# Causal scores in 64x64 tiles without their empty blocks: what it does to a retention and expert kernel

## The chip, the cores and the metric

The kernel runs on one core of one Trainium2 chip. The metric is the device time of one execution in microseconds (us). Three runs of the kernel before took 401.07, 401.35 and 401.92 us; the median is 401.35.

## The reference, cut to what matters

Retention (linear attention with a decay per head) is followed by a mixture of experts with one expert per token. Only the retention is touched by the change.

```
B, H, S, D = 4, 8, 768, 64
gamma = 1 - 2 ** (-5 - arange(H)); scale = 1 / sqrt(D)
for t in range(S):
    state = gamma * state + k[:, :, t] (outer) v[:, :, t]
    y[:, :, t] = scale * q[:, :, t] @ state
...
x = y as (3072 tokens, 512)
expert of a token = argmax(x @ w_gate + bias of its modality)
out = gate * relu(x @ w1[expert]) @ w2[expert]
```

Within a stretch of 128 tokens, y of token t is the part that comes from the state before the stretch, and the sum over the tokens s <= t of the stretch of (q_t . k_s) v_s with decays. The matrix of these scores is zero for s > t: a causal mask.

## The kernel before, in words

The 3072 tokens are 24 chunks of 128 (six per batch, so chunk n starts a batch where n % 6 == 0 and ends one where n % 6 == 5). All operands are fp32; an fp32 matmul is two instructions on TensorE (PE). For each chunk the kernel runs these steps, all with 8 heads of 64, held as 4 groups g of two heads j:

- `load_kq`, `load_kv` (L119 to L140): 512 KB each, q and k with features on the partitions, and k and v with tokens on the partitions. SyncE (SP) issues them some ten chunks ahead.
- `decay_v` (L152): v times a decay on GpSimd (POOL). `decay_q` (L142): a decay for the output on ScalarE (ACT), four instructions.
- `scores` (L161): k^T q for each head, a 64x128 tile (64 rows of the array, 128 columns) with 128 moving columns, into two PSUM banks, one for each j; then VectorE (DVE) multiplies each bank by the mask and writes it to `abuf` (L173).
- `heads_s` (L183): the state's part of y, 64x64 tiles (L192). `heads_a` (L197): the scores' part, added in the same PSUM tiles, 128x64 tiles with 128 moving columns (L204); then DVE writes `yT` (L211).
- `tokens_out` (L213): y back to token rows and the gate logits in one matmul with 128x128 tiles (L221), copied by ACT to `xs` (L225), logits summed by DVE into `lg` (L226).
- `state` (L230): k^T v added to the state in a PSUM tile that lives as long as the batch, 128x64 tiles (L240), copied by ACT.

PSUM has 8 banks here, all from one pool with one tag (`bank`, L78); a new tile takes a bank whose last tile is released, and waits until that tile's readers are done. PE, ACT, DVE and SP run their instructions in the order in which the program writes them (`manual_schedule`, L1055).

The order around the change: `one_chunk` handles chunks 0 and 1, `first_pair` prepares chunks 2 and 3, and `two_chunks(n)` (L899) handles n and n+1 for n = 2, 4, ... 22. In it the scores and the state of the next pair are made, and `tokens_out` of the last pair. Other work is put between the steps by hooks (`at`, `run`): `run(n, "end")` after the tokens, for example, runs what was put there.

- In chunks 6, 12 and 18, at "end": `route_a` parts 0 and 1 (L312), the routing of the six chunks before, a row of small DVE instructions (L316 to L340).
- In chunks 7, 13 and 19, at "end": `route_b`, `route_c`, `route_a` part 2 (rank matmul, positions, gates), in 13 also `early_a` and `early_b` (L455 to L487: DVE picks the two experts that start early).
- In the two chunks after that, six `scatter`s on POOL (L366), one instruction after the other, each with an indirect DMA.
- In chunk 14: `taken_a` at "st" (DVE writes `tk`), `taken_b` at "end" (PE matmuls `ptk`, L497, that read `tk`).
- In chunks 18 and 20, at "end": `cut` (L669), a weight block split in two by ACT (`hi_e`) and DVE (`lo_e`, L677). In chunks 20 and 22: `flip`, transposes on PE for the first expert job.

After the attention, six jobs of experts follow (`first` L692, `second` L711), 192 matmuls of 128x512 each.

## Time and profile before

| What | Before |
|---|---|
| Median of three runs | 401.35 us |
| Profiled execution | 402.62 us, of which span 400.8 us |
| PE busy | 383.6 us, 96% of the span |
| DVE, ACT, POOL busy | 47%, 39%, 24% |
| Scores on PE (L168) | 27.7 us, 384 instructions, mean 293 ns |
| Scores' part of y on PE (L204) | 27.5 us, 384 instructions, mean 290 ns |
| Mask product on DVE (L173) | 30.0 us, 48 instructions, mean 681 ns |
| First expert matmul (L698) starts | 111.87 us |

Times in a timeline are microseconds from the start of the span. Matmuls are pipelined, so one instruction's length (some 0.3 us) is much longer than the step from one to the next. A row of the timeline gives the start, the length of the whole block, engine, line, operation, what is written from what, the tile form as rows*columns of the array, the shape of the moving operand and the count; in brackets, the idle time before it and what ended that. In the answer on stretches of the span, each engine has its busy time and, in parentheses, its instruction count; then come the clock granted to PE, the share of the DMA engines and GB/s.

### The profile page before, as it was taken

The page shows a single profiled execution, that of the slowest core. Times are in us where ns is not written, and L with a number is a line of the kernel's source. Part 1 is how long each engine was busy: PE and PEld are TensorE (multiplying, and loading weights), DVE is VectorE, ACT ScalarE, POOL GpSimd, SP SyncE. Part 2 cuts the span into 40 slices and gives each one's busy share as a digit, 9 for nine tenths or more (in the row PEclk, how much of TensorE's full clock was granted, in tenths as well). Part 3 has the DMA queues.
Part 4 walks back from the last instruction along what each step waited for, and adds up shares of the span by engine and source line. Part 5 has one row for each costly group of instructions (what it writes and reads, how often), then busy time and mean ns, then how long its engine had stood idle before and what let it go on. Part 6 is the DMA issues. An engine that isn't in the chain of part 4 may idle for free.

```text
span 400.8 us, 8169 instructions
## 1 busy us (share of the span) xinstructions
PE 383.6 (96%) x3067; PEld 323.2 (81%) x3067; DVE 187.8 (47%) x434; ACT 155.6 (39%) x305; POOL 96.7 (24%) x140
## 2 busy tenths in 40 slices
PE   4999999799999999999999999999999999999993
PEld 3999888698887888888877888878888888888882
DVE  1676858768649952445223352233622463234200
ACT  1255535336845432345223452334523443243110
POOL 1342581832810875000110001100011000100010
PEclk9999999899999999999999999999999999999999
DMA  7999899794545759367952579525343443400011
GB/s 273 398 385 398 303 339 400 239 390 174 198 147 189 248 184 330 116 216 243 370 201 81 198 243 359 214 71 199 105 159 105 156 166 131 151 35 0 15 39 50
DMA packets 27947, 82.32 MB, mean 205 GB/s; under 512 B 4861, under 2 KB 4989, under 8 KB 27649
## 3 DMA queue, kind: packets, MB, share of 16 engines
q1 hardware_dynamic: 22336, 66.09, 47.4%
q0 software_dynamic: 5136, 15.21, 9.8%
q8 instruction: 26, 0.43, 0.4%
q10 hardware_dynamic: 432, 0.46, 0.4%
q14 instruction: 17, 0.14, 0.1%
HBM read 65.42 MB, written 23.41 MB: 222 GB/s over the span
## 4 chain that ended last, share of the span: by engine, by line
PE 46%; issue 32%; DMA 12%; POOL 4%; DVE 3%; ACT 1%; POOLq 1%; SPq 0%; ACTq 0%
PE h_e L698 11%; PE o_e L716 11%; DMA kq<-in_qkv_dram 6%; DMA kv<-in_qkv_dram 6%; PE h_f L698 6%; PE o_f L716 5%; PE x L221 4%; POOL out_dram L730 3%; PE y L204 2%; PE sc L168 2%; PE y L192 1%; PE st L240 1%; PE xp_f L683 1%; PE xp_e L683 1%; DVE yT L211 1%
## 5 line engine op out<-in xcount | busy, mean ns | idle before, releaser
L698 PE MATMUL h_f<-xT_f,hi_f 128*128 128x512 f32 x256 | 81.3, 393 | 0.0
L716 PE MATMUL o_f<-hi_f,hT_f 128*128 128x512 f32 x256 | 79.4, 391 | 0.0
L677 DVE TENSOR_TENSOR lo_f<-raw_f,hi_f 128x1024 fp32r<-128x1024 f32 x32 | 39.2, 1224 | 49.5 <-ACT hi_f L672 45.3
L698 PEld LDWEIGHTS h_f<-xT_f,hi_f 128*128 128x128 f32 x256 | 48.1, 188 | 11.1 <-issue 1.2
L716 PEld LDWEIGHTS o_f<-hi_f,hT_f 128*128 128x128 f32 x256 | 47.6, 188 | 9.6
L706 DVE SCALAR_TENSOR_TENSOR hT_f<-h_f,hT_f 128x512 fp32r<-128x512 f32 x32 | 22.2, 692 | 66.4 <-ACT hT_f L705 66.4
L698 PE MATMUL h_f<-xT_f,lo_f 128*128 128x512 f32 x128 | 49.9, 390 | 0.0
L716 PE MATMUL o_f<-lo_f,hT_f 128*128 128x512 f32 x128 | 49.9, 390 | 0.0
L730 POOL DMA_INDIRECT out_dram<-o_f,tok_f x16 | 15.6, 972 | 132.6 <-ACT o_f L729 117.8
L698 PE MATMUL h_e<-xT_e,hi_e 128*128 128x512 f32 x128 | 40.5, 392 | 0.0
L705 ACT ACTIVATE hT_f<-h_f 128x512 fp32r<-128x512 f32 x32 | 19.2, 599 | 54.9 <-PE h_f L698 54.9
L716 PE MATMUL o_e<-hi_e,hT_e 128*128 128x512 f32 x128 | 39.8, 392 | 0.0
L173 DVE TENSOR_TENSOR abuf<-sc,cst 128x512 f32<-128x512 f32 x48 | 30.0, 681 | 17.4 <-PE sc L168 17.4
L156 POOL TENSOR_TENSOR vd<-kv,cst 128x512 f32<-128x512 f32 x24 | 24.9, 1045 | 42.5 <-PE y L204 13.5
L672 ACT CAST hi_f<-raw_f 128x1024 fp32r<-128x1024 f32 x32 | 33.4, 1045 | 0.0
L168 PE MATMUL sc<-kq 64*128 64x128 f32 x384 | 27.7, 293 | 5.4 <-DMA kq<-in_qkv_dram 5.2
L729 ACT ACTIVATE o_f<-o_f,gate_f 128x512 f32<-128x512 f32 x15 | 10.3, 689 | 55.0 <-PE o_f L716 43.6
L168 PEld LDWEIGHTS sc<-kq 64*128 64x128 f32 x384 | 24.6, 199 | 7.3 <-DMA kq<-in_qkv_dram 5.2
L221 PE MATMUL x<-wgt,yT 128*128 128x136 f32 x192 | 26.6, 287 | 3.1 <-DVE abuf L173 2.9
L225 ACT COPY xs<-x 128x272 f32<-128x272 f32 x48 | 18.4, 388 | 26.3 <-PE x L221 18.8
L716 PEld LDWEIGHTS o_f<-lo_f,hT_f 128*128 128x128 f32 x128 | 24.0, 188 | 5.0
L698 PEld LDWEIGHTS h_e<-xT_e,hi_e 128*128 128x128 f32 x128 | 24.0, 188 | 4.9
(172 smaller groups left out, 536.7 us busy)
## 6 DMA issues: line engine op xcount, KB each, us to landing
raw_f<-in_w_dram SPq DMA_DIRECT2D x32, 512.0 KB, 3.5
kq<-in_qkv_dram SPq DMA_DIRECT2D x23, 512.0 KB, 8.1
kv<-in_qkv_dram SPq DMA_DIRECT2D x19, 512.0 KB, 9.6
raw_e<-in_w_dram SPq DMA_DIRECT2D x16, 512.0 KB, 4.4
xg_f<-xsl SPq DMA_DIRECT2D x16, 272.0 KB, 4.4
abuf<-in_w_dram SPq DMA_DIRECT2D x8, 512.0 KB, 6.8
rw<-in_w_dram SPq DMA_DIRECT2D x16, 256.0 KB, 5.4
xg_e<-xsl SPq DMA_DIRECT2D x8, 272.0 KB, 4.2
```

The lines of the kernel that those rows point to most:

```text
L156: nc.gpsimd.tensor_tensor(vds[n], vv, dec[:, n % NCH].unsqueeze(2).to_broadcast([P, H, D]), op=ALU.mult)
L168: nc.tensor.matmul(pe[j][:, g * P : (g + 1) * P], kt[r, g], qt[r, g], start=True, stop=True, skip_group_check=True,)
L173: nc.vector.tensor_tensor(a[:, j], pe[j].rearrange("p (h t) -> p h t", t=P), mask.unsqueeze(1).to_broadcast([P, NG, P]), op=ALU.mult,)
L221: nc.tensor.matmul(px[:, g], yT[:, 2 * u + g], wgt[:, 2 * u + g], start=(g == 0), stop=(g == 1), skip_group_check=True,)
L225: nc.scalar.copy(xs[:, 2 * u : 2 * u + 2], px)
L672: nc.scalar.copy(hi, t)
L677: nc.vector.tensor_tensor(lo, t, hi.bitcast(F32), op=ALU.subtract)
L698: nc.tensor.matmul(s.ph, s.w[1][f // 2][wi][:, o : o + P], s.xT[kc][a], start=(kc == 0 and k == 0), stop=(kc == KC - 1 and k == 2),)
L705: nc.scalar.activation(hi, s.ph, AF.Relu)
L706: nc.vector.scalar_tensor_tensor(lo, s.ph, 0.0, hi.bitcast(F32), op0=ALU.max, op1=ALU.subtract)
L716: nc.tensor.matmul(s.po, s.hT[f][a][:, hh * P : (hh + 1) * P], s.w[2][f // 2][wi][:, (f % 2) * DM : (f % 2 + 1) * DM], start=(f == 0 and k ...
L730: ins = nc.gpsimd.indirect_dma_start(out=out[:, :], out_offset=bass.IndirectOffsetOnAxis(ap=s.tok[:, hh : hh + 1], axis=0), in_=o[:, :], i ...
```

## The change

Each head's 128x128 score matrix is cut into 64x64 blocks; the block of late k and early q is zero and is no longer made. For one head, k's early half gives 64 rows with 128 columns, k's late half 64 rows with 64 columns. So that the two heads of a pair of groups fill a bank together, some heads (`turned`) have their token halves exchanged: on the partitions of the scores, and in v, k and the decays with tokens on the partitions, which the host lays out so. Two heads share 192 columns (`AW`): 64 columns with the early blocks of both (low), then 64 for each head with all 128 rows (high). The mask product has 2 x 192 columns in place of 512. The scores' part of y is then made in two steps: `heads_lo`, 64x64 tiles with 64 columns, and `heads_hi`, 128x64 tiles with 64 columns. Heads are placed differently in the y tiles (partition half by g // 2, column by g % 2), and constants and gate weights follow.

[...]

The order of `two_chunks` changes: both `scores` move behind `tokens_out` and the hooks at "end"; the second one stands between the first and the second half of `heads_lo`. The forms of PE's tiles in a pair are then 128x128, 64x64, 128x64; before they were 64x128, 128x128, 64x64, 128x64.

```diff
     def scores(n):
         kt, qt = (kqs[n][:, i].rearrange("p (g t) -> p g t", g=NG) for i in range(2))
...
+        for late in range(2):
+            for u in range(2):
+                for j in range(2):
+                    r = slice(j * D, (j + 1) * D)
+                    for g in (2 * u, 2 * u + 1):
+                        w = turned(g, j)
+                        o = pe[j][(late + w) % 2 * HP : ((late + w) % 2 + 1) * HP, u]
+                        qs = qt[r, g]
...
+                        nc.tensor.matmul(
+                            o, kt[r, g, late * HP : (late + 1) * HP], qs,
+                            start=True, stop=True, skip_group_check=True,
+                        )
         for j in range(2):
             nc.vector.tensor_tensor(
+                a[:, j], pe[j], mask.unsqueeze(1).to_broadcast([P, 2, AW]), op=ALU.mult
             )
...
+    def heads_lo(n, c):
...
+        for j in range(2):
+            for g in (c, c + 2):
+                w = turned(g, j)
+                r = slice(w * HP, (w + 1) * HP)
+                h = slice(g // 2 * D, (g // 2 + 1) * D)
+                ins = nc.tensor.matmul(
+                    py[j][h, c, :HP], vd[r, 2 * g + j], a[r, j, g // 2, :HP],
+                    start=(first and c == 0), stop=(c == 1), skip_group_check=True,
+                )
+                if c and seen:
+                    tc.add_manual_dep(ins.ins, seen.pop().ins.name, synced, reason="PSUM banks")
+
+    def lo_seen(n):
+        seen.append(nc.scalar.copy(sight, pys[n][1][HP : HP + 1, 0, :1]))
+
+    def heads_hi(n):
...
+        for j in range(2):
+            for g in (0, 2, 1, 3):
+                w = turned(g, j)
+                h = slice(g // 2 * D, (g // 2 + 1) * D)
                 nc.tensor.matmul(
+                    py[j][h, g % 2, HP:], vd[:, 2 * g + j],
+                    a[:, j, g // 2, (1 + w) * HP : (2 + w) * HP],
+                    start=False, stop=(g % 2 == 1), skip_group_check=True,
                 )
...
@@ two_chunks
         decay_q(n)
-        if ahead:
-            scores(n + 2)
         run(n, "st")
         if ahead:
-            scores(n + 3)
             decay_v(n + 3)
...
             tokens_out(n - 1)
-        decay_q(n + 1)
         run(n, "end")
         run(n + 1, "top")
+        if ahead:
+            scores(n + 2)
         if n % NCH:
             heads_s(n)
+        heads_lo(n, 0)
         heads_s(n + 1)
+        heads_lo(n + 1, 0)
+        lo_seen(n + 1)
         run(n + 1, "st")
-        heads_a(n)
+        decay_q(n + 1)
+        if ahead:
+            scores(n + 3)
+        heads_lo(n, 1)
+        heads_lo(n + 1, 1)
+        heads_hi(n)
+        heads_out(n)
+        run(n + 1, "sc")
         if ahead:
             state(n + 2)
-        run(n + 1, "sc")
-        heads_a(n + 1)
+        heads_hi(n + 1)
+        heads_out(n + 1)
         run(n + 1, "pr")
         if ahead:
             state(n + 3)
@@ one_chunk
         state(n)
         decay_q(n)
         run(n, "st")
-        scores(n + 1)
...
             heads_s(n)
-        heads_a(n)
+        heads_lo(n, 0)
+        lo_seen(n)
+        scores(n + 1)
+        heads_lo(n, 1)
+        heads_hi(n)
+        heads_out(n)
         run(n, "end")
```

`heads_out` holds the two DVE instructions that write yT. `heads_s` keeps its matmuls and goes through the groups as 0, 2, 1, 3.

## The prediction

> **What bounds the kernel now.** I read the page first, then the stretches of the span, the waits before TensorE (PE), and PE's timeline of one pair of chunks.

> ```profile
> PE 383.6 (96%) x3067; PEld 323.2 (81%) x3067; DVE 187.8 (47%) x434; ACT 155.6 (39%) x305; POOL 96.7 (24%) x140
> 120.00:200.00 80.00, 80.00 (x373) 65.98 (x372) 42.88 (x112) 32.46 (x47) 25.81 (x33) 1.00 0.69 237
> 20.00:30.00 10.00, 10.00 (x178) 9.21 (x178) 7.46 (x15) 5.77 (x19) 4.72 (x6) 1.00 1.02 385
> PE sc L168 <- DMA kq<-in_qkv_dram: 5.2, 1, 5.2
> PE x L221 <- DVE abuf L173: 2.9, 1, 2.9
> kq<-in_qkv_dram SPq DMA_DIRECT2D x23, 512.0 KB, 8.1
> ```

> PE is busy for 96% of the span, and for all of 120 to 200 us in the experts' stage, so a microsecond that attention wins or loses reaches the end whole. Its one wait for a load is the first; the queues are then full (a share of 1.02 at 385 GB/s), but a pair needs two chunks of two 512 KB loads, 5.4 us, which still fits under a pair of 7. Its longest wait for another engine is 2.9 us, on VectorE (DVE). So I price PE's work first, and then ask which waits the new order makes.

> ```profile
> 26.27 2.06 PE L168 MATMUL sc<-kq 64*128 64x128 f32 x32
> 28.26 2.12 PE L221 MATMUL x<-wgt,yT 128*128 128x136 f32 x16
> 30.31 1.10 PE L192 MATMUL y<-kq,s 64*64 64x128 f32 x32
> 31.34 1.09 PE L204 MATMUL y<-abuf,vd 128*64 128x128 f32 x16
> 33.60 0.64 PE L240 MATMUL st<-vd,kv 128*64 128x64 f32 x16
> 34.17 0.38 PE L168 MATMUL sc<-kq 64*128 64x128 f32 x2
> ...
> 18.06 1.16 PE L168 MATMUL sc<-kq 64*128 64x128 f32 x16
> 19.15 1.19 PE L221 MATMUL x<-wgt,yT 128*128 128x136 f32 x8
> 38.20 0.67 PE L192 MATMUL y<-kq,s 64*64 64x128 f32 x16
> 109.03 1.97 PE L204 MATMUL y<-abuf,vd 128*64 128x128 f32 x32
> 64.20 0.63 PE L240 MATMUL st<-vd,kv 128*64 128x64 f32 x16
> L240 PE MATMUL st<-vd,kv x320: 219/222/369, 8.0 to 103.7; 128*64 128x64 f32 x160
> ```

> The columns are start, length, line, tile form (rows*columns of the array), moving operand and count; each fp32 matmul is two instructions. A block's length includes its first fill and last drain, so rates come from differences. Scores: 2.06-1.16 = 0.90 us for 16 more, a chunk. Tokens: 2.12-1.19 = 0.93 for 8. The state's part of y (L192): 1.10-0.67 = 0.43 for 16, so a round of four 64x64 tiles with 128 columns takes 0.1075. The scores' part of y (L204): 1.97-1.09 = 0.88 a chunk. State (L240): the last of 16 lasts 0.222, so (0.63-0.222)/7 = 0.058 for a round of two with 64 columns, 0.465 a chunk.

> One pair takes 34.17-26.27 = 7.90. Its work is 2 x 0.90 + 1.86 + 2 x 0.43 + 2 x 0.88 + 2 x 0.465 = 7.21. The other 0.69 lies at four changes of tile form: 0.17 each.

> **PE's work after.** A chunk's scores become four rounds of four 64x64 tiles with 128 columns and four with 64: 4 x 0.1075 + 4 x t. No row has 64x64 tiles with 64 columns. Low bound for t: 0.058, L240's round of two 128x64 tiles, which holds as many weights as four 64x64. High bound: 0.1075, if 16 instructions never go faster than in L192. I take the low one, since instructions of different tiles start almost together:

> ```profile
> 30.31 0.34 PE L192 MATMUL y<-kq,s 64*64 64x128 f32 x4
> ```

> Four that last 0.32 or 0.33 each fit into 0.34 us, so issue does not space them by 27 ns. Scores then cost 0.66, down 0.24. The scores' part of y becomes four such rounds (0.23) and eight of L240's kind (0.465): 0.70, down 0.18. Over 24 chunks: 0.42 x 24 = 10.1 us less. The forms go from four to three a pair, and in the second single chunk: 11 x 0.17 = 1.9. PE's work shrinks by 12.0 us. The reordered loop of L192 and the renamed halves cost nothing: as many instructions, the same tiles.

> [...]

> **Smaller parts.** The mask product has 384 columns instead of 512:

> ```profile
> 35.36 2.48 DVE L173 TENSOR_TENSOR abuf<-sc,cst 128x512 f32<-128x512 f32 x4 [1.05 <-PE sc L168]
> 41.94 0.74 DVE L211 TENSOR_TENSOR yT<-y,dcq 128x256 f32<-128x256 f32 x2
> ```

> With 0.60 between starts for 512 columns and 0.33 for 256, about 0.47, some 0.55 in length. decay_q(n+1) moves behind ACT's new copy, and yT(n+1), which uses it, comes only after the high parts. The larger constants and the extra memset fall into the first microseconds, ahead of their users. The new one-element ScalarE (ACT) copy makes PE wait before the second half of the low part; behind it stands all of PE's queue. It costs 0.24 (next row, 48 columns), after 0.22 until PE's result is there; the scores put between take 0.66, so it is covered, except in the last pair, which has none: 0.4, and 0.3 more there for yT, which has only one chunk's high part as cover.

> ```profile
> L321 ACT ACTIVATE ex<-lg 128x48 f32<-128x48 f32 x4 | 0.9, 236 | 1.9 <-DVE lg L319 1.9
> ```

> **The wait that the new order makes.** Eight PSUM banks: the state keeps one, and the y tiles of both chunks, taken before scores(n+3), keep four. Three are left, last used by a token tile and by the two tiles of scores(n+2). So scores(n+3) needs at least one bank that DVE's mask product of chunk n+2 must first read. That banks are waited for in this way shows here:

> ```profile
> 73.41 0.73 PE L221 MATMUL x<-wgt,yT 128*128 128x136 f32 x4 [2.88 <-DVE abuf L173]
> 96.53 1.49 PE L168 MATMUL sc<-kq 64*128 64x128 f32 x16 [0.20 <-DVE yT L211]
> ```

> Before, both chunks' scores came ahead of tokens_out and of the hooks at "end". Now these hooks precede scores(n+2) in DVE's order. In an ordinary pair that is harmless. In pairs 6, 12 and 18 the hook is the routing:

> ```profile
> 30.83 0.21 DVE L226 TENSOR_REDUCE lg<-xs 128x8 f32<-128x32 f32 x1 [0.72 <-ACT xs L225]
> 38.73 0.21 DVE L226 TENSOR_REDUCE lg<-xs 128x8 f32<-128x32 f32 x1 [0.72 <-ACT xs L225]
> 40.17 0.97 DVE L330 TENSOR_TENSOR oh<-iota3m,mn 128x48 bf16<-128x48 f32 x1
> 40.04 1.04 POOL L156 TENSOR_TENSOR vd<-kv,cst 128x512 f32<-128x512 f32 x1 [5.13 <-PE y L204]
> L330 DVE TENSOR_TENSOR oh<-iota3m,mn 128x48 bf16<-128x48 f32 x4 | 3.1, 784 | 0.1
> ```

> The last lg starts 30.83-28.26 = 2.57 after the tokens' start; from it to the product behind the routing are 41.94-38.73 = 3.21. L330's 0.97 falls on GpSimd's (POOL's) product; of the four only three are long, so alone it takes 0.2. POOL's product waits for PE's y, which now comes after the routing: 3.21-0.77 = 2.44. The mask product then starts at 2.57+2.44 = 5.01 and ends at 5.56. PE is at scores(n+3) after tokens 1.86+0.17, scores 0.66, low parts 2 x 0.12 and one state part 0.43: 3.36. PE waits 2.2 us, in pairs 6 and 12 (3.0 if L330 stays long). In pairs 18 and 20 a weight cut stands there too:

> ```profile
> 97.95 0.66 PE L683 MATMUL xp_e<-cst,xg_e 128*128 128x128 f32 x4
> 101.20 0.56 PE L192 MATMUL y<-kq,s 64*64 64x128 f32 x12
> 101.30 0.39 ACT L225 COPY xs<-x 128x272 f32<-128x272 f32 x1 [0.17 <-PE x L221]
> 102.77 1.03 ACT L672 CAST hi_e<-raw_e 128x1024 fp32r<-128x1024 f32 x1
> 103.83 1.23 DVE L677 TENSOR_TENSOR lo_e<-raw_e,hi_e 128x1024 fp32r<-128x1024 f32 x1 [1.33 <-ACT hi_e L672]
> ```

> Pair 18: 1.14 more, a wait of 3.3. Pair 20: flips and tokens take 3.25, the last xs ends 3.74 in, then 1.03, 1.2 and 0.55: 6.5, against PE's 3.25+0.66+2 x 0.43+0.23 = 5.0: 1.5, of which some 0.8 is lost there already (0.20; 0.33 of 1.49; rest at the tokens). In pair 14 the 2.9 us wait stays under another name:

> ```profile
> 67.75 0.19 DVE L360 TENSOR_TENSOR rkt<-rk,oh 128x48 f32<-128x48 f32 x1
> 72.69 1.27 DVE L173 TENSOR_TENSOR abuf<-sc,cst 128x512 f32<-128x512 f32 x2
> ```

> The list of early jobs takes DVE 4.94, then tk 0.17; PE's ptk matmul comes 2.0 into the pair and waits some 3.3 (+0.4). POOL's chain of scatters ahead of decay_v does not shrink with PE:

> ```profile
> 56.69 0.69 PE L240 MATMUL st<-vd,kv 128*64 128x64 f32 x16 [0.82 <-POOL vd L156]
> ```

> I add 0.6 to this 0.82: the two pairs that the chain runs beside shrink by some 0.9 each (so 0 to 1.8), but the routing that starts it ends earlier too. Waits: 2.2 + 2.2 + 3.3 + 0.7 + 0.4 + 0.6 + 0.7 = +10.1.

> **The clock.** After the 2.88 us wait the granted clock fell:

> ```profile
> 75.07:78.48 3.41, 3.41 (x48) 3.08 (x42) 1.43 (x7) 0.81 (x4) 2.62 (x7) 0.50 0.86 220
> ```

> Half a clock for 3.41 us costs 1.7. The waits of 3.3 should each bring one, of the two of 2.2 I take one: three in place of one, +3.4 (0 to +5.1). [...]

> **Sum.** -12.0 + 10.1 + 3.4 = +1.5, less some 0.4 for small waits in the old order: +1.1. The profiled execution has 402.6 us, 1.8 outside its span, and lies 1.3 above the median of 401.35; from the median this gives 402.5, about no change, with a range of its own of 399 to 406 (waits of 2.2 or 3.0, none to four half clocks).

> **Rivals.** (1) DVE does not hold the banks: scores(n+3) gets others, or the product runs ahead of the routing. Against: the count of banks; DVE kept the written order throughout the trace. Then 8.4 us of waits and at least 2 us of clock go: 391 (389 to 395). (2) Slower: 64-column 64x64 tiles keep L192's 27 ns apiece (t = 0.1075) from the first scores on. That adds 0.05 x 8 x 24 = 9.5, of which some 2 goes into the waits above, and as these shorten one half clock less: 408 (406 to 411). It decides once t is over 0.07. For: no row shows a lasting rate above L192's; against: the four starts. (3) The ACT copy comes too late because token copies or a dq stand ahead of it on ACT: up to 0.4 in each of 12 pairs, 406.

> **Numbers.** Forecast 0.56, rival 1 0.24, rival 2 0.13, rival 3 0.07. A measurement tells 0.2%, 0.8 us, from no change. The forecast's case, spread over 399 to 406, gives faster 0.17, same 0.14, slower 0.25; rival 1 is all faster, 2 and 3 nearly all slower. Together faster 0.42, same 0.15, slower 0.43. The range leaves out most of rival 1 and the upper end of rival 2: 392 to 408.5.

> **What the new profile would show.** Scores blocks of 0.66 and pairs 8 and 16 near 7.0 or below; scores rows in pairs 6, 12 and 18 waiting over 2 us on DVE's abuf; a ptk row waiting over 3 us on tk; stretches at clock 0.50 behind them. Wrong if pairs 6 and 18 are shorter than before (rival 1), or if scores blocks keep 0.85 (rival 2).

## The result, and the profile after

The changed kernel takes 415.19 us, the median of 415.16, 415.18, 415.21 and 416.57; the kernel before, beside it, 401.55 us. The ratio is 1.0349, with a 95% interval of 1.0324 to 1.0373: slower by some 13.6 us, where 402.5 was forecast, with a range up to 408.5.

Two rows of the page after, its first part (busy time of each engine) and its list of DMA queues:

```profile
PE 378.1 (91%) x3835; PEld 320.2 (77%) x3835; DVE 179.0 (43%) x435; ACT 155.9 (38%) x318; POOL 96.3 (23%) x140
...
q8 instruction: 32, 0.52, 0.5%
```

and the same queue on the page before:

```profile
q8 instruction: 26, 0.43, 0.4%
```

PE is busy for less time (378.1 against 383.6 us), but for 91% of the span and not 96%: the time went into gaps. Its matmuls and its weight loads each rose from 3067 to 3835, and the instruction queue carried 32 packets in place of 26, 16 KB each. The loss lies in the attention. The first expert matmul (the tile h_e) shows where that ends; the last two times are its first and its last start:

```profile
L750 PE MATMUL h_e<-xT_e,hi_e x128: 388/390/498, 126.0 to 194.8; 128*128 128x512 f32 x128
```

It started at 111.87 us before and starts at 126.0 now, 14.1 later; the experts then take as long as before. The waits of PE in the attention (total, times, longest):

```profile
PE sc L192 <- DVE abuf L197: 8.0, 4, 2.9
PE sc L192 <- DMA kq<-in_qkv_dram: 5.3, 1, 5.3
PE y L231 <- issue: 4.4, 2, 2.6
PE x L272 <- issue: 3.3, 2, 1.7
PE ptk L549 <- DVE tk L543: 3.3, 1, 3.3
PE y L249 <- issue: 2.3, 1, 2.3
PE y L215 <- issue: 1.7, 2, 1.4
...
PE y L231 <- ACT sight L240: 0.3, 1, 0.3
```

Two kinds matter beside the first load, which is as before. The waits for VectorE (8.0 and 3.3 us) are those that were forecast. The four rows with "issue", 11.7 us in all, are new: PE waits there for nothing that the profile's rows name. They cut through blocks of one kind of matmul, where no other engine has anything to deliver (timeline of PE):

```profile
25.73 1.20 PE L272 MATMUL x<-wgt,yT 128*128 128x136 f32 x9
28.68 0.86 PE L272 MATMUL x<-wgt,yT 128*128 128x136 f32 x6 [1.74 <-issue]
...
31.96 0.35 PE L231 MATMUL y<-abuf,vd 64*64 64x64 f32 x9
34.95 0.49 PE L231 MATMUL y<-abuf,vd 64*64 64x64 f32 x7 [2.63 <-issue]
35.37 1.12 PE L249 MATMUL y<-abuf,vd 128*64 128x64 f32 x16
...
63.19 0.22 PE L249 MATMUL y<-abuf,vd 128*64 128x64 f32 x1
65.67 0.62 PE L249 MATMUL y<-abuf,vd 128*64 128x64 f32 x14 [2.25 <-issue]
```

Row five shows the second loss. The heads' high part takes 1.12 us there; the same block takes 0.69 elsewhere. From the second of the two waits before it, PE ran at half clock for 6.8 us (stretch of the span; the third number from the end is the granted clock, then the DMA share and GB/s):

```profile
34.38:41.20 6.83, 6.25 (x81) 6.01 (x81) 1.70 (x4) 1.13 (x3) 2.09 (x2) 0.50 1.02 403
```

Counting PE's weight loads, matmuls and semaphore instructions in order of start, the longer waits on "issue" sit at these places. The packets are those of the instruction queue in the trace's list of DMA packets; one takes 0.9 to 1.2 us.

```
number in PE's queue   last before   goes on at   packet began
 706 = 2*256 + 194       21.75         22.36         19.92
 962 = 3*256 + 194       26.66         28.68         26.33
1218 = 4*256 + 194       32.10         34.95         32.48
2242 = 8*256 + 194       58.37         60.05         57.84
2498 = 9*256 + 194       63.19         65.67         63.20
3522 = 13*256 + 194      91.25         93.25         90.87
3778 = 14*256 + 194      97.52         99.39         96.84
```

A matmul is four instructions here, two weight loads and two passes (the scores before: 384 of each for 24 chunks of 8 heads). A pair has 16 matmuls of scores, 8 of tokens, 16 and 16 of y, and 16 of state: 72, or 288 instructions. In the changed kernel scores have 32 and y 48: 104, or 416. Before, 256 instructions lasted 6.2 to 7.9 us in the full stretches, about as long as a block needs, and PE stood for 0.15 us at most. Now the blocks that end in such a wait hold 3.2 to 5 us of work.

### The profile page after: what moved, and what is told of

It is laid out like the page before. It is cut to its first block, busy times and chain, and to the rows that moved or that the text cites. A ratio compares the mean times of both kernels' runs of the same rounds, so it can differ in the third digit from the quotient of the medians.

```text
span 414.8 us, 9723 instructions
## 1 busy us (share of the span) xinstructions
PE 378.1 (91%) x3835; PEld 320.2 (77%) x3835; DVE 179.0 (43%) x435; ACT 155.9 (38%) x318; POOL 96.3 (23%) x140
## 4 chain that ended last, share of the span: by engine, by line
PE 53%; issue 34%; DVE 4%; DMA 3%; POOL 3%; ACT 1%; POOLq 1%; ACTq 0%; SPq 0%
PE h_e L750 11%; PE o_e L768 11%; PE h_f L750 5%; PE x L272 5%; PE o_f L768 5%; PE sc L192 3%; PE y L249 3%; POOL out_dram L782 3%; PE st L291 3%; DMA kv<-in_qkv_dram 2%; PE y L215 2%; PE y L231 1%; DMA cst<-in_consts_dram 1%; PE xp_e L735 1%; PE xp_f L735 1%
## 5 line engine op out<-in xcount | busy, mean ns | idle before, releaser
L192 PE MATMUL sc<-kq 64*64 64x64 f32 (+1 forms) x768 | 25.2, 264 | 13.3 <-DVE abuf L197 8.0
L197 DVE TENSOR_TENSOR abuf<-sc,cst 128x384 f32<-128x384 f32 x48 | 24.4, 552 | 25.0 <-PE sc L192 25.0
L192 PEld LDWEIGHTS sc<-kq 64*64 64x64 f32 x768 | 21.4, 145 | 15.5 <-DVE abuf L197 8.9
L272 PE MATMUL x<-wgt,yT 128*128 128x136 f32 x192 | 28.0, 296 | 3.4 <-issue 3.3
L272 PEld LDWEIGHTS x<-wgt,yT 128*128 128x128 f32 x192 | 25.1, 201 | 4.6 <-issue 3.6
## 6 DMA issues: line engine op xcount, KB each, us to landing
raw_f<-in_w_dram SPq DMA_DIRECT2D x32, 512.0 KB, 3.4
kq<-in_qkv_dram SPq DMA_DIRECT2D x23, 512.0 KB, 7.4
kv<-in_qkv_dram SPq DMA_DIRECT2D x19, 512.0 KB, 9.3
raw_e<-in_w_dram SPq DMA_DIRECT2D x16, 512.0 KB, 4.7
abuf<-in_w_dram SPq DMA_DIRECT2D x8, 512.0 KB, 6.1
```

Source lines behind the costliest of these rows:

```text
L192: nc.tensor.matmul(o, kt[r, g, late * HP : (late + 1) * HP], qs, start=True, stop=True, skip_group_check=True,)
L197: nc.vector.tensor_tensor(a[:, j], pe[j], mask.unsqueeze(1).to_broadcast([P, 2, AW]), op=ALU.mult)
L272: nc.tensor.matmul(px[:, g], yT[:, 2 * u + g], wgt[:, 2 * u + g], start=(g == 0), stop=(g == 1), skip_group_check=True,)
```

## The experiments

Theory 1: instruction supply, as above. Theory 2: the 64x64 tiles or the new order make the waits on "issue". Theory 3: they cost nothing, and the waits for VectorE are the loss. Runs made together share a chip and runs of the kernel before, to which ratios refer. The changed kernel took 415.19 us on one chip and 420.92 on another, so its variants on different chips compare to some 6 us at best.

**The number of instructions alone.** In the kernel before, each matmul of the scores and their part of y is issued in two halves:

```diff
+                for f in (slice(0, D), slice(D, P)):
                     nc.tensor.matmul(
-                        pe[j][:, g * P : (g + 1) * P], kt[r, g], qt[r, g],
+                        pe[j][:, g * P : (g + 1) * P][:, f], kt[r, g], qt[r, g][:, f],
```

> The kernel before, its order and tile forms kept; each matmul of the scores and of their part of y is issued as two of half the columns (64). A pair then issues 416 instructions on TensorE, as many as the changed kernel, where the kernel before has 288; the columns to stream stay the same. Theory 1 (instruction supply: TensorE's instructions arrive in blocks of 256, one packet of 16 KB of the instruction queue each, and while the load queues are full such a block takes some 6 us to arrive, longer than 256 of these instructions last): waits on nothing (issue) of over 1 us appear, at least four of them between 20 and 70 us, all a multiple of 256 TensorE instructions apart; 408 to 414 us. Theory 2 (the 64x64 tiles or the new order make these waits) and theory 3 (only the waits for VectorE matter): no such waits, 400 to 403 us.

Measured: 428.6 us (four runs from 422.46 to 430.17), with one wait on issue, of 1.4 us, at a multiple of 256 too. The experiment missed its aim, since PE's work did not stay the same (timeline):

```profile
60.01 1.20 PE L206 MATMUL y<-abuf,vd 128*64 128x64 f32 x32
...
62.54 3.72 PE L169 MATMUL sc<-kq 64*128 64x64 f32 x62
```

62 scores instructions of 64 columns take 3.72 us, where before 32 of 128 columns took 2.06: halving the columns saved nothing in these tiles, whose weights are 128 columns wide. (The halves of one head now follow each other, where before the two heads in the two halves of the array's rows took turns and started in twos, 7 ns apart; whether the weights' width or this made it was not tested.) L206, with 64 weight columns, keeps its length (1.20 for 32; 1.09 for 16 of twice the columns before). With PE that much slower the instructions keep up. So the next one splits both matmul groups of y, whose weights are 64 columns wide:

```diff
+                for f in (slice(0, D), slice(D, P)):
                     nc.tensor.matmul(
-                        py[j][h, g // 2], s[r, g], qv[r, g], start=(g < 2), stop=False,
+                        py[j][h, g // 2, f], s[r, g], qv[r, g, f],
+                        start=(g < 2 and f.start == 0), stop=False,
```

> The kernel before, its order and tile forms kept; this time both matmul groups of y (the state's and the scores' part) are issued as two of half the columns, 416 instructions a pair as in the changed kernel. Unlike the scores, whose 64x128 tiles took as long for 64 columns as for 128 in the first split (51.8 us for all scores instead of 25.4), these tiles are 64 weight columns wide, and in the first split the scores' part of y cost 24.6 instead of 23.9 us with twice the instructions; so TensorE's work should stay as it was. Theory 1 (instruction supply): waits on issue of 1 to 2.6 us, at least four between 20 and 70 us, a multiple of 256 TensorE instructions apart; 408 to 416 us. Theory 2 (64x64 tiles of the scores or the order make them) and theory 3: no such waits, 400 to 404 us.

Measured: 419.1 us, 1.0391 (1.0327 to 1.0454). Waits:

```profile
PE y L206 <- issue: 3.9, 5, 2.8
PE sc L168 <- issue: 3.5, 2, 3.3
```

The two long waits (2.8, 3.3) stand at instructions 1218 and 2498, 5 x 256 apart, as in the changed kernel, though tiles, order and columns are those of before; a half clock sets in as each ends (behind the first a granted clock of 0.52 from 37.3 to 40.8 us). Two long ones, not four. By steps from start to start, the waits at multiples of 256 are some 7 of the 17 us lost, one more half clock 1.7, and 11 short stops at other places some 4; such stops were seen on three of the chips only (last section). The rest is slower steps. The same without the loads of chunks 4 to 23 (edit further below):

> The split of both parts of y (416 instructions a pair, old order and tiles, 419.1 us) with the loads of chunks 4 to 23 left out. Theory 1: twice the instructions cost time only while the load queues are full; the waits on issue at multiples of 256 (3.0 and 3.6 us the longest) go, and it comes near the quiet kernel before (404.93): 405 to 411 us. If the doubled instructions cost TensorE that much by themselves: 418 to 423 us.

Measured: 406.99 us. The three longest rows:

```profile
PE sc L174 <- DMA kq<-in_qkv_dram: 5.1, 1, 5.1
PE x L230 <- DVE abuf L179: 2.4, 1, 2.4
PE st L249 <- POOL vd L162: 0.8, 2, 0.6
```

No wait on issue is left. So the added instructions cost some 17 us beside full load queues and 2 us beside quiet ones (406.99 against 404.93, below). The quiet run was on another chip, which showed none of the short stops; without these the 17 is some 13. Theories 2 and 3 can't say why.

**Quiet queues in the changed kernel.**

```diff
     def load_kq(n, split=False):
+        if n >= 4:
+            kqs[n] = kqs[n % 4]
+            return
```

and the same in `load_kv`.

> The changed kernel without the loads of chunks 4 to 23: these chunks compute from the inputs of chunk n mod 4, so the output differs; TensorE's program is the same. From about 16 us on the queues carry only the stores and the weights. Theory 1 (instruction supply delayed by the full load queues): the waits on issue before 90 us go, and the half clock at 34 to 41 us with them; the waits for VectorE stay; 398 to 405 us. Theory 2 (tiles or order) and a fourth theory (blocks of 256 take that long to arrive whatever the queues carry): the waits on issue stay, 412 to 416 us.

> Control for the quiet run: the kernel before without the loads of chunks 4 to 23 (the output differs in the same way). Theory 1: the kernel before hardly waits for instructions, so quiet queues give it little: 398 to 402 us, and the 7 us by which the quiet changed kernel (407.97) stands above it are the waits for VectorE, GpSimd and the early list's matmul, less the work saved. If quiet queues speed the kernel before by 5 us or more, the loads cost something else too.

Measured: 407.97 us, and 404.93 us for the kernel before. Of PE's waits in the changed kernel remain

```profile
PE sc L198 <- DVE abuf L203: 7.9, 4, 2.9
...
PE st L297 <- POOL vd L164: 3.3, 3, 1.3
PE ptk L555 <- DVE tk L549: 2.7, 1, 2.7
PE st L297 <- issue: 0.8, 1, 0.8
```

and the attention ends at

```profile
L756 PE MATMUL h_e<-xT_e,hi_e x128: 388/389/497, 114.3 to 183.7; 128*128 128x512 f32 x128
```

```profile
L704 PE MATMUL h_e<-xT_e,hi_e x128: 387/389/497, 112.2 to 181.7; 128*128 128x512 f32 x128
```

The waits on issue are nearly gone (11.7 to 1.1 us), those for VectorE are not. The longer one left, of 0.8 us, stands at a multiple of 256 as well, at 77.6 us, where the DMA share is 0.96 again (72 to 78 us). The attention's loss falls from 14.1 to 2.1 us. (The two were on different chips. Both lose some 3 us behind the attention, probably because the experts get other tokens; this was not followed up.) A half clock came back at another place, at 38.6 us (0.51 from there to 42.1 us), behind a wait of 1.80 for VectorE.

**Order and tiles apart.** The kernel before with the order of the change alone, and the changed kernel with the order of before:

```diff
 two_chunks (order alone)
         run(n + 1, "top")
+        if ahead:
+            scores(n + 2)
...
+        decay_q(n + 1)
+        if ahead:
+            scores(n + 3)
         heads_a(n)
```

> The kernel before with the new order alone: both chunks' scores behind the hooks at end, scores(n+3) behind heads_s, decay_q(n+1) later; old tiles, 288 instructions a pair. Theory 1 (instruction supply): no wait on issue of over 0.7 us; waits of scores(n+3) for VectorE's abuf of about 2 us in pairs 6 and 12, 3 in pair 18, 1.4 in pair 20; 406 to 412 us. Theory 2 (the order makes the waits on issue): they appear as in the changed kernel, 414 to 420 us. Theory 3 (only the VectorE waits made the loss): as theory 1, but then the changed kernel's whole loss of 13.6 us plus the work saved has to be found here, 420 us or more.

> The changed kernel with its new tiles in the order of before: scores of both chunks ahead of the token tiles and the hooks; the small ScalarE copy has no scores to cover it. Theory 1 (instruction supply): waits on issue of 1 to 2.6 us stay, five or more before 100 us, a multiple of 256 TensorE instructions apart; the waits of the scores for VectorE's abuf go; 404 to 411 us. Theory 2 in the form that the order makes them, and theory 3: the waits on issue go or cost nothing, 390 to 397 us.

Measured: 404.74 us, 1.0091 (1.0062 to 1.0119), for the order; 413.95 us, 1.0307 (1.0263 to 1.035), for the tiles. PE's waits with the order alone:

```profile
PE ptk L495 <- DVE tk L489: 3.6, 1, 3.6
PE y L202 <- DVE abuf L173: 1.9, 3, 1.4
PE sc L168 <- DVE abuf L173: 1.1, 1, 1.1
```

and with the tiles in the old order:

```profile
PE sc L192 <- issue: 6.3, 4, 2.4
PE y L231 <- ACT sight L240: 6.1, 11, 2.0
...
PE y L215 <- issue: 1.5, 2, 1.3
PE y L249 <- issue: 1.2, 1, 1.2
PE y L231 <- issue: 0.9, 1, 0.9
```

The order makes no wait on issue; the tiles have them in either order (11.7 us in the new, 9.9 in the old). With the order alone the waits for abuf are smaller than expected (3.0 us): in pairs 6 and 12 scores(n+3) does not wait, and the scores' part of y waits 0.27 us in each. Why the banks fall otherwise was not followed up. The ScalarE copy, uncovered here, cost 6.1 us in 11 pairs (whether it is needed no run shows); in the changed kernel only the last pair waits for it (0.3).

**VectorE's waits removed.** The second part of the routing, the early list's matmul and the cuts move behind the mask products:

```diff
-        at(t, "end", route_a, g, 1)
+        at(t + 1, "sc", route_a, g, 1)
...
-    at(t + 2, "end", taken_b)
+    at(t + 3, "end", taken_b)
...
-        at(t + 6 + 2 * i, "end", cut, e, 1, i)
-        at(t + 7 + 2 * i, "top", raw, e, 2, i)
+        at(t + 7 + 2 * i, "sc", cut, e, 1, i)
+        at(t + 7 + 2 * i, "pr", raw, e, 2, i)
```

> The changed kernel with VectorE's long steps moved behind the mask products: the second part of the routing behind the first of yT, the early list's matmul one chunk later, the two weight cuts (and the loads behind them) into the next chunk. Theory 1: the scores' waits for VectorE's abuf (8.0 us in all) fall to under 3, the early list's wait (3.3) too; the waits on issue stay at 9 us or more, and in the stretch to 70 us, where TensorE runs at the pace of its instructions, part of the saved wait comes back as longer waits on issue; 405 to 412 us. Theory 3 (the VectorE waits are the loss): 396 to 402 us.

Measured: 415.66 us. It had no changed kernel beside it, so both were run together on another chip:

> The changed kernel unchanged, beside the other three of this call, as their control: 413 to 418 us, waits on issue of 10 to 14 us.

> The moved hooks once more, now beside the changed kernel. Theory 1 (TensorE is held by its instruction supply as soon as VectorE does not hold it): within 4 us of the control. If the two kinds of waits simply add up: 7 to 10 us below the control.

Measured: 420.92 and 418.66 us. The changed kernel's waits, and those with the hooks moved:

```profile
PE sc L192 <- DVE abuf L197: 7.7, 4, 2.9
...
PE x L272 <- issue: 4.9, 4, 2.0
PE y L231 <- issue: 4.2, 5, 2.6
PE ptk L549 <- DVE tk L543: 3.3, 1, 3.3
PE y L249 <- issue: 2.6, 5, 1.3
```

```profile
PE st L291 <- issue: 3.3, 3, 2.5
PE x L272 <- issue: 2.9, 2, 2.0
PE y L231 <- issue: 2.1, 4, 1.1
PE sc L192 <- DVE abuf L197: 2.0, 3, 1.6
...
PE y L249 <- issue: 1.8, 5, 0.4
```

Nine microseconds of waits for VectorE are gone, and 2.3 us are won, so theory 3 falls. Where the nine went is only in part known. At 48.07 and 75.38 us PE now waits (2.7 and 1.4 us, from start to start) at multiples of 256 where it did not before: it seems that a block which had arrived during a wait for VectorE is now waited for. But all waits on issue together stay as they were (12.6 and 12.0 us); fewer stand at multiples of 256 and more elsewhere. Waits for the later routing, 1.4 us of them at the matmul of its ranks, come on top.

> The moved hooks and the quiet queues together (loads of chunks 4 to 23 left out, as in the quiet run). Each alone: hooks moved 415.66, no gain; quiet 407.97, with the quiet kernel before at 404.93. Theory 1 (TensorE is held either by VectorE or by its instruction supply, and where one wait goes the other takes its place): together both go; waits on issue under 2 us, the scores' waits for abuf under 3 us; 397 to 402 us, below the quiet kernel before, and attention ends at 104 to 108 us. If moving the hooks costs something of its own (which would also explain 415.66): 405 to 408 us, no better than the quiet run.

Measured: 408.38 us, 1.014 (1.011 to 1.0169): a miss, no better than the quiet kernel with its hooks in place. The waits on issue of over 1.5 us are gone, but many short ones stand in their place (6.4 us on issue in all; section on the hardware). They appeared on this chip and two others, and not on that of the quiet run, so the two can't be set against each other, and a cost of the moved hooks themselves is not excluded.

**Can the blocks be made to come earlier?** Rings of 8 chunk buffers; loads in two halves; at most three loads on their way, with SP waiting for the third last:

```diff
 rings of 8
-LEAD = 12
+LEAD = 8
-        tag = f"{('hi', 'lo')[n // 4 % 2]}{1 if n < 8 else 2}{n % 4}"
+        tag = f"{('hi', 'lo')[n // 4 % 2]}2{n % 4}"
...
-        tag = f"xT{n - 8}" if n // 4 == 2 else f"hT{(n if n < 8 else n - 12) % 8}"
+        tag = f"hT{n % 8}"
 halves
-            nc.sync.dma_start(t, qkv[n][:, 0:2])
+            nc.sync.dma_start(t[:, 0], qkv[n][:, 0])
+            nc.sync.dma_start(t[:, 1], qkv[n][:, 1])
 few at a time
+        if len(asked) >= 3:
+            tc.add_manual_dep(ins.ins, asked[-3].ins.name, synced, reason="few at a time")
```

> The changed kernel with rings of 8 chunk buffers in place of up to 20, loads 8 chunks ahead in place of 12: the same bytes, spread over more of the stage, the queues less full from 20 to 70 us and fuller after. Theory 1: the waits on issue before 70 us (9.7 us) shrink to 2 to 6, some appear after 80 us; 408 to 414 us, and the half clock at 34 to 41 us goes in part. Theory 4 (a block takes as long whatever the queues carry) and theory 2: the waits on issue stay as they are, 414 to 417 us.

> The changed kernel with each load of a chunk's keys and queries, or keys and values, as two of half the size: packets of 2 KB (84 ns each) in place of 4 KB (159 ns), the same bytes, twice the issues. Under full queues an instruction packet starts 3 to 4.5 us after it is wanted. Theory 1a (it stands behind a number of load packets, some 22 of 159 ns): the delay falls to about 2 us, the waits on issue to under 4 us, 402 to 408 us. Theory 1b (it stands behind a number of bytes, or its delay has nothing to do with the packets' size): no change, 413 to 418 us.

> Control: the kernel before with half-size loads. It does not wait for instructions (the new blocks come within 0.15 us), so theories 1a and 1b both expect 399 to 404 us; a change beyond that would mean that the load size matters in another way.

> The changed kernel, with each load of a chunk asked for only when the third last one has landed: at most 3 x 512 KB on their way in place of 8. Theory 1c (an instruction packet stands behind the loads that are already on their way): the delay of 3 to 4.5 us falls to about 2, the waits on issue to under 5 us, 402 to 409 us. Theory 1d (a full queue shares its engines in turn, however many loads stand in it): the delay stays as long as loads run without a break, 412 to 418 us; if the loads become too slow for TensorE, waits for kq or kv show it, and it is slower.

Measured: 424.27 us; 422.36 us; 404.75 us, 1.0053 (1.0034 to 1.0071); 422.18 us beside 420.92. None helps. Smaller buffers were to ease the queues before 70 us and did not: the DMA share from 20 to 40 us is 1.02, against 1.01 in the changed kernel, the last load is issued at 92 us in place of 86, and the waits on issue are 13 us. Packets of half the size leave the delay at mostly 2 to 4 us. With three loads on their way it falls to 2 to 3.4 us and the waits on issue to 8.0, but nothing is won: the clock is halved at five places in the attention, and the loads run at 288 GB/s early in it, where they had up to 405. What orders an instruction packet among the loads stays open; their number matters some, their packets' size little at most.

With the hooks moved as well:

> Moved hooks and half-size loads together, the candidate for a version that beats both kernels. Theory 1a: 394 to 400 us. Theory 1b: as with the moved hooks alone, 413 to 418 us.

> Moved hooks and at most 3 loads on their way, the candidate for a version that beats both kernels. Theory 1c: 395 to 402 us. Theory 1d: 410 to 416 us.

Measured: 417.44 and 417.49 us.

**A version that beats both.** None of these variants pays for the tiles, but the half clock can be had back in the kernel before: the second early list is made one hook later.

```diff
-            at(t + 1, "end", early_b, g + 1)
             a, b = EARLY[g + 1]
+            at(t + 1, "end", early_b, g + 1, (a,))
+            at(t + 2, "end", early_b, g + 1, (b,))
...
-    at(t + 2, "st", taken_a)
-    at(t + 2, "end", taken_b)
+    at(t + 3, "st", taken_a)
+    at(t + 3, "end", taken_b)
```

> A version meant to beat both kernels, as the tiles can't be paid for: the kernel before, with the second of the two early lists made one hook later (behind pair 14's token tiles in VectorE's order, its matmul one chunk later). The kernel before waits 2.88 us there for VectorE's mask product, behind which 3.41 us at half clock follow (1.7). If nothing takes their place: 396 to 398.5 us. If another wait does (yT of chunk 14 behind the second list): 400 to 402 us.

Measured: 398.04 us, 0.992 (0.9906 to 0.9934): 0.8% faster, a small but clear gain. Pair 14's tokens, before cut in two by 2.88 us (timeline), and the stretch around them:

```profile
68.70 2.39 PE L221 MATMUL x<-wgt,yT 128*128 128x136 f32 x16
71.02 1.79 PE L192 MATMUL y<-kq,s 64*64 64x128 f32 x32
```

```profile
66.00:80.00 14.00, 13.65 (x210) 11.94 (x212) 11.85 (x45) 7.58 (x24) 9.46 (x20) 1.00 0.93 311
```

The tokens run through, and the clock is 1.00 where it had been 0.50. The first expert matmul starts at 107.9 us, 4.0 earlier than before, of the 4.6 that the wait and its half clock were worth (2.88 and 1.7). With 288 instructions a pair no wait for a block took the place of this one.

## Why the prediction was wrong

**PE's work: right.** Adding up the steps from one matmul's start to the next, those over 0.28 us counted as waits, the attention has 98.4 us of work before and 92.0 after. Half clock, for four times 3.41 us in place of once, cost about 5.1 of it, so the saving at full clock is some 11.5, against 12.0 forecast. A chunk's scores (at 29.47) are followed 0.72 us later by the next block, against 0.66 and up to 0.17 for the change of form. Inside it the rounds of four 64x64 tiles with 64 columns start 0.058 us apart (30.011, 30.070, 30.128), the very t that was taken, and rival 2 falls. Pair 8, without a wait, took 6.42 us from tokens to tokens, below the 7.0 forecast; pair 16, forecast alike, took 9.14 with a wait on issue in it.

**VectorE's waits: right, a little too high.** Forecast for the scores in pairs 6, 12, 18 and 20: 2.2, 2.2, 3.3 and 1.5; measured 1.80, 1.80, 2.94 and 1.41. The early list: some 3.3, measured 3.33. The last pair's ACT copy: 0.4, measured 0.3. Rivals 1 and 3 fall with these rows. GpSimd's wait, forecast to grow by 0.6, did not (1.6 before, 1.4 after). By steps, all waits but those on issue grew by 7.4 us, against 9.7 forecast.

**The failing step** is the one on how fast instructions issue: "Four that last 0.32 or 0.33 each fit into 0.34 us, so issue does not space them by 27 ns". That holds for four, and for as many as have arrived. The sum had no term for where they come from. Its 128 more instructions a pair were priced by their work alone, and the page's row for the instruction queue (0.4% of the DMA time) was not read. The prediction even said that loads keep the queues full (1.02) while "a pair needs ... 5.4 us, which still fits under a pair of 7": the same full queues delay the instructions. A pair's 416 instructions are 1.6 blocks; at the 5.1 to 6.9 us that a block took beside full queues they need 8.3 us or more, and not 7. The 288 of before are 1.1 blocks and fit into the 7.9 us that a pair took. What the runs showed in its place: 11.7 us of waits on issue, nearly gone with quiet queues (attention +2.1, near the +1.1 forecast), made in the old kernel too by adding instructions alone, and there a loss of 17 us (some 13 without the short stops) beside full queues against 2 beside quiet ones.

**The clock: short by one, and half of it for another reason.** Three stretches of 3.41 us at half clock were forecast; four such lengths came, two of them in one piece. The two behind the waits of 2.9 and 3.3 us for VectorE are the forecast ones; the third forecast, behind one of the scores' waits in pairs 6 and 12 (now 1.80), did not come. The double one, from 34.4 us, sets in during a wait on issue. So the forecast causes gave +1.7 of the +3.4 forecast, and waits on issue another +3.4; that forecast and measured clock lie near each other is luck.

In sum, by steps: -11.5 of work, +5.1 for the clock, +7.4 for the other waits and +13.1 for those on issue make +14.1, as much as the first expert matmul starts later. (The 13.1 counts from the start of the last matmul before a wait; the 11.7 of the rows counts from its modelled end.)

## What to carry to other kernels

Count the instructions of a stage beside its work: smaller tiles that save columns multiply instructions. Here PE was through 256 of them in 3.2 to 5 us, and beside full load queues it could go on only 5.1 to 6.9 us after they began. Where gaps put down to "issue" cut through a uniform block, number the engine's instructions and see whether the gaps are a fixed count apart, as here by multiples of 256. And waits in a row on one engine need not add up (nine microseconds of them went here, and 2.3 were won): when one goes, see which takes its place before counting the gain.

## What the runs showed of the hardware

- In the changed kernel seven waits of PE on "issue", of 0.6 to 2.9 us from start to start, stood multiples of 256 PE instructions apart, and PE went on 2.2 to 2.6 us after a 16 KB packet of the instruction queue began, itself 0.9 to 1.2 us long. Counted from the start of the 256 instructions before, the packets of the attention began mostly 3 to 4.5 us later beside full load queues (DMA share 0.99 to 1.03), and mostly from 0.3 us before to 1.5 us after it in the changed kernel with quiet ones.
- In the first split a 64x128 tile took as long for 64 moving columns as for 128 (51.8 and 25.4 us for all scores, added up by steps, with twice the instructions and another order of the heads), a 128x64 tile about half as long (1.20 us for 32 instructions, 1.09 for 16).
- On three of the chips, not on the one first measured, PE also stopped for 0.3 to 0.7 us in the pairs in which POOL issues its six scatters, in the middle of a block and not at a multiple of 256 (timeline of the changed kernel beside the moved hooks):

```profile
53.01 0.56 PE L249 MATMUL y<-abuf,vd 128*64 128x64 f32 x10
53.95 0.37 PE L249 MATMUL y<-abuf,vd 128*64 128x64 f32 x5 [0.37 <-issue]
...
55.61 0.47 PE L249 MATMUL y<-abuf,vd 128*64 128x64 f32 x9 [0.36 <-issue]
```

Most of these stops began 0.7 to 1.0 us after a scatter did (at 52.66 and 54.26 us here). The changed kernel took 420.92 us there and 415.19 on the first, the kernel before 401.5 on both. Their cause was not settled, and as each chip was used on one occasion, that it is the chip is not shown either.
